# Loading a pair's keys and values: two 64-partition transfers, or one over 128 partitions and a small one for the tail

## The chip, the cores and the metric

The kernel runs on one core of one Trainium2 chip. The metric is the device time of one execution in microseconds (us), the median of several runs; lower is better. Engines are named as in the profile: PE (TensorE matmuls), PEld (its weight loads), DVE (VectorE), ACT (ScalarE), POOL (GpSimd), SP (SyncE, which issues every DMA here).

## What is computed

Two stages. The first is linear attention over 8 batches of 8 heads, 576 tokens and head dimension 64; its normed output, with the heads side by side, is the input x of the second, a gated feed-forward block with a spatial mixing of the 576 tokens.

```python
kv = np.einsum('bhsd,bhse->bhde', k, v)
out = np.einsum('bhsd,bhde->bhse', q, kv)
rms = np.sqrt(np.mean(out * out, axis=-1, keepdims=True) + 1e-06)
x = heads_side_by_side(out / rms * g_norm)         # 8 x 576 x 512

h = np.maximum(x @ w_in, 0.0)                      # 512 -> 1024
u, v = h[..., :512], h[..., 512:]
v_n = (v - mu) / np.sqrt(var + 1e-06)              # over the 512
v_s = np.einsum('ts,bsd->btd', w_spatial, v_n) + b_spatial[None, :, None]
out = (u * v_s) @ w_out                            # 512 -> 512
```

All inputs are float32 except `w_in` and `w_out`, which come as 64-bit floats.

## The kernel before

**Attention.** Heads go in pairs (`p`, four to a batch), so that a pair fills 128 columns. 576 tokens are four chunks of 128 (`NC = 4`) and a tail of 64 (`TAIL`). `att_load` (L97) brings a pair's keys and values into one of two `KV` buffers of shape `[P, 2, NC + 1, P]`: key or value, chunk, column. The fifth chunk is the tail in partitions 0 to 63, with zeros in 64 to 127 set once at the start. The host lays the tail beside the four chunks for partitions 0 to 63 (`kvlo`, 320 KB a pair) and leaves the four chunks alone for 64 to 127 (`kvhi`, 256 KB), so a pair takes two transfers of 64 partitions each; the very first pair takes four, in two pieces. `att_k` (L116) forms the 64x64 product of each head of the pair in ten matmuls (five chunks, two heads) into `pskv` and copies it to `KVB` (even batches) or `KVO` (odd ones). `att_qa` multiplies it with the queries (`qt`, or `qs` for the tail rows), `norm_a` and `norm_b` are the RMS norm (line 169 its sums, line 174 its product), `att_t` transposes to `XH` and its rounding rest `XL`. The tails of two batches are handled together (`pst`, `pstt`).

**Feed-forward.** All big products are float32r in a high and a low part, so three matmuls each. `hv_k`/`hv_end` make `v` (`psh`), normalise it and split it into `VH`, `VL` with the sums (L312 to L315) that a Strassen-like spatial product needs; `u_unit` makes `u` (`psu`, evicted by ACT into `U` at L343); `sp_steps` is the spatial product with the gate (`psa`, `psb`, `psc`), `out_unit` the last product. `psh`, `psu`, `psa`, `psb` and `psc` share four banks.

**Weights** are loaded to `stage` buffers and split: `weight64` (L484) with ACT, DVE and POOL for `w_in` and `w_out` (to `WIH`, `WIL`, `WOH`, `WOL`), `make_ws` and `make_tail` for `wsT`, the transposed spatial weights (to `WSH`, `WSL`, `WTH`, `WTL`). POOL works in pieces of 144 columns.

**Order.** Over the first two batches the order is written out by hand in `PLAN` (W loads a weight, C converts one, L loads the next of the attention's inputs, K and J are `att_k`, A/D and B the norm's two halves, T transposes, H one step of `psh`, u a `psu` unit, s a spatial step). Later batches interleave attention steps of the batches to come with the feed-forward of this one. The kernel is built with a scheduler that orders each engine's instructions by its own estimate of times, so instructions move where an estimate changes. At most two pairs' keys are in flight (`issue`, L569), and all DMAs are issued by SP in order.

Of the kernel before, what the change touches and what calls it, by code (L numbers as in the profile page):

```python
# [8 lines left out]
F32 = mybir.dt.float32  # L9
# [7 lines left out]
B, H, S, D = 8, 8, 576, 64  # L17
DM, FF = 512, 1024
FH = FF // 2
P = 128  # L20
NP = H // 2
NC = S // P
TAIL = S - NC * P
# [20 lines left out]


@with_exitstack
def body(ctx: ExitStack, tc, qT, kvlo, kvhi, g2, w_in, wsT, bsp, w_out, out):
    nc = tc.nc
    w_in = w_in.bitcast(U32)
    w_out = w_out.bitcast(U32)  # L50
# [9 lines left out]
    def persistent(shape, dt, name):  # L60
        return const.tile(shape, dt, name=name, tag=name)
# [21 lines left out]
    KVO = [persistent([P, P], F32, f"KVO{i}") for i in range(NP)]  # L83


    KV = [persistent([P, 2, NC + 1, P], F32, f"KV{i}") for i in range(2)]
    ident = persistent([P, P], F32, "ident")
    gcol = persistent([P, 1], F32, "gcol")
    epsc = persistent([P, 1], F32, "epsc")
# [4 lines left out]
    keys, queries = {}, {}  # L94
    n_load = [0]

    def att_load(b, p, kind):  # L97
        if kind in "fk":
            kv = KV[n_load[0] % 2]
            n_load[0] += 1  # L100
            for i, j in ((0, 2), (2, NC + 1)) if (b, p) == (0, 0) else ((0, NC + 1),):
                nc.sync.dma_start(kv[0:TAIL, :, i:j], kvlo[b, p, :, :, i:j])
                j = min(j, NC)
                nc.sync.dma_start(kv[TAIL:P, :, i:j], kvhi[b, p, :, :, i:j])
            keys[b, p] = kv, None
        if kind == "k":
            qs = load.tile([P, P], F32, name="qs", tag="qs")
            nc.sync.dma_start(qs, qT[b, p, :, S - P:S])
            keys[b, p] = kv, qs
        else:  # L110
            n = S if kind == "f" else NT
            qt = load.tile([P, S], F32, name="qt", tag="qt")
            nc.sync.dma_start(qt[:, 0:n], qT[b, p, :, 0:n])
            queries[b, p] = qt

    def att_k(b, p, st, copy=nc.vector.tensor_copy):  # L116
        kv, qs = keys.pop((b, p))
        ps = ps_att.tile([P, 512], F32, name="pskv", tag="att")

        for c in range(NC + 1):  # L120
            for h in slice(0, D), slice(D, P):
                nc.tensor.matmul(ps[h, h], kv[:, 0, c, h], kv[:, 1, c, h],  # L122
                                 start=c == 0, stop=c == NC)
        st[p] = KVO[p] if b % 2 else KVB[p % 2]
        copy(st[p][0:D, 0:D], ps[0:D, 0:D])
        nc.scalar.copy(st[p][D:P, D:P], ps[D:P, D:P])
        if qs is not None:
            att_end(p, st, qs)
        issue()

    def att_end(p, st, q):

        if p == 0:
            st["tail"] = ps_tail.tile([P, 512], F32, name="pst", tag="tail")
        nc.tensor.matmul(st["tail"][:, p * P:(p + 1) * P], q, st[p], start=True, stop=True)  # L135
# [92 lines left out]
    def att_steps(b):  # L228

        st = states.setdefault(b, {})  # L230

        def loading(f):
            return lambda: (f(), ahead())

        def t2():
            att_t(b, 2, st)
            tail_a(b, st)
            tail_b(b, st)

        def tail():  # L240
            tail_a(b, st)
            tail_b(b, st)

        K = [lambda p=p: att_k(b, p, st) for p in range(NP)]
        Q = [loading(lambda p=p: att_q(b, p, st)) for p in range(NP)]
        T = [lambda p=p: att_t(b, p, st) for p in range(NP)]
        end = lambda: att_tail(b, st)
        if b % 2 == 0:
            return [K[0], K[1], Q[0], K[2], Q[1], T[0], K[3], Q[2], T[1], Q[3], t2, T[3], end], []
        return [loading(k) for k in K] + [tail, end], [Q[0], Q[1], T[0], Q[2], T[1], Q[3], T[2],  # L250
                                                       T[3], move_tail]
# [317 lines left out]
    def issue():  # L569

        while wanted[0] and todo and (len(queries) if todo[0][2] == "q" else len(keys)) < 2:
            wanted[0] -= 1
            att_load(*todo.pop(0))
# [6 lines left out]
    nc.vector.memset(epsc, EPS)  # L580
    nc.scalar.activation(small.tile([P, 1], F32, name="warm", tag="av"), epsc, AF.Sqrt)
    nc.gpsimd.memset(KVB[0], 0.0)
    for kv in KV:
        nc.gpsimd.memset(kv[TAIL:P, :, NC, :], 0.0)
    for kvb in KVO:
        nc.gpsimd.memset(kvb, 0.0)
    make_identity(nc, ident)
# [32 lines left out]
    def conv():  # L620
# [12 lines left out]
        "N": warm,  # L633
        "L": lambda: ahead(), "W": lambda: loads.pop(0)(), "C": conv, "S": step,
        "K": lambda b, p: att_k(b, p, st[b]), "A": lambda b, p: att_qa(b, p, st[b]),
        "B": lambda b, p: att_qb(b, p, st[b]), "T": lambda b, p: att_t(b, p, st[b]),
        "J": lambda b, p: att_k(b, p, st[b], nc.scalar.copy),
        "D": lambda b, p: att_qa(b, p, st[b], True), "d": lambda b: tail_a(b, st[b], True),
        "a": lambda b: tail_a(b, st[b]), "b": lambda b: tail_b(b, st[b]),
# [95 lines left out]
```

## Time and profile before

| | |
|---|---|
| median of 3 runs | 540.55 us (537.82 to 540.96) |
| span of the profiled execution | 538.6 us; no other time is given for it, and the median lies 1.95 us above the span |
| PE busy | 510.0 us, 95% of the span |
| DVE, ACT, POOL busy | 370.7, 247.1, 92.8 us |
| DMA | 46.7 MB, 31.6% of 16 engines' span |
| keys and values | 31 issues each of 320.0 KB (5.4 us to landing) and 256.0 KB (5.8 us), beside the first pair's four smaller ones |

Busy time is the time in which an engine executes. Idle time of an engine counts only where another waits for it. The granted PE clock is a share of full speed. The table of stretches gives for each piece of the span the busy time of every engine; a timeline row gives start, duration, engine, line, operation, out<-in, and in brackets the idle time before it with what ended it.

### The profile page before, as it was taken

Reading aid. Unit: us, or ns where it says so; the run is one execution under the profiler, and the core shown is the slowest. Engines: PE = TensorE matmul, PEld = TensorE weight load, DVE = VectorE, ACT = ScalarE, POOL = GpSimd, SP = SyncE. Lnnn points to the kernel's source line nnn. Section 1 sums busy time; section 2 is a strip of 40 time slices with the busy share of each in tenths; the row PEclk is TensorE's granted clock in tenths of the full one; section 3 lists DMA queues with packets and bytes.
Section 4 is the critical chain, followed back from the end, with each engine's and each line's share of the span. In section 5 each row is a group of like instructions: output and inputs, shape, how many; then the busy total and the mean of one; then the engine's idle time right before and its main releaser. Section 6 shows DMA issues by size and latency. Waiting matters only on the chain.

```text
span 538.6 us, 9728 instructions
## 1 busy us (share of the span) xinstructions
PE 510.0 (95%) x3568; PEld 459.2 (85%) x3568; DVE 370.7 (69%) x1086; ACT 247.1 (46%) x645; POOL 92.8 (17%) x181
## 2 busy tenths in 40 slices
PE   6958787999999999999999999999999999999997
PEld 5747776989897899989998799978998789988995
DVE  2898879888494497918585289928577089947470
ACT  4675864355442356425444256424444256434421
POOL 7699995323000000000000000000000000000000
PEclk7896798999999999999999999999999999999999
DMA  8995412062517401120733800120451500010002
GB/s 232 289 297 127 115 39 63 22 175 58 153 34 178 116 2 40 44 79 2 158 101 86 211 21 21 44 79 0 116 135 50 157 8 12 21 60 19 2 2 97
DMA packets 22344, 46.68 MB, mean 87 GB/s; under 512 B 2900, under 2 KB 5460, under 8 KB 22296
## 3 DMA queue, kind: packets, MB, share of 16 engines
q1 hardware_dynamic: 22296, 46.06, 31.6%
q8 instruction: 28, 0.46, 0.4%
q14 instruction: 20, 0.16, 0.1%
HBM read 36.61 MB, written 9.44 MB: 85 GB/s over the span
## 4 chain that ended last, share of the span: by engine, by line
PE 80%; DMA 10%; DVE 5%; POOL 1%; SPq 1%; issue 1%; ACT 1%; POOLq 0%; DVEq 0%
PE psu L258 19%; PE pso L258 16%; PE psh L288 15%; PE psb L352 6%; PE pso L182 4%; PE psa L352 4%; PE psc L352 4%; PE pskv L122 4%; DMA KV<-kvlo 3%; DMA KV<-kvhi 3%; DMA stage<-w_in 2%; PE pstr L210 2%; PE psh L258 2%; DMA stage<-wsT 1%; PE pst L135 1%
## 5 line engine op out<-in xcount | busy, mean ns | idle before, releaser
L258 PE MATMUL psu<-XH,WIH 128*128 128x288 f32 x256 | 77.7, 304 | 3.6 <-ACT U L343 3.6
L258 PE MATMUL psu<-XL,WIH 128*128 128x288 f32 x256 | 76.4, 299 | 0.0
L258 PE MATMUL psu<-XH,WIL 128*128 128x288 f32 x256 | 76.2, 299 | 0.0
L258 PE MATMUL pso<-WOH,GH 128*128 128x512 f32 x144 | 59.1, 410 | 0.1
L226 POOL CAST XL<-XL 128x256 fp32r<-128x256 f32 x4 | 2.0, 507 | 324.0 <-PE psu L258 324.0
L258 PE MATMUL pso<-WOL,GH 128*128 128x512 f32 x144 | 57.1, 396 | 0.0
L379 ACT CAST GH<-g 128x288 fp32r<-128x288 f32 (+2 forms) x96 | 30.0, 351 | 53.3 <-DVE g L371 48.8
L258 PE MATMUL pso<-WOH,GL 128*128 128x512 f32 x144 | 54.4, 397 | 0.0
L267 DVE BATCH_NORM_STATS2 s<-v 128x6 f32<-128x512 f32 x36 | 24.7, 691 | 42.7 <-ACT v L264 42.5
L258 PEld LDWEIGHTS psu<-XH,WIH 128*128 128x128 f32 x256 | 49.1, 192 | 4.7 <-ACT U L343 3.9
L288 PE MATMUL psh<-WIH,XH 128*128 128x512 f32 x128 | 51.7, 404 | 0.0
L288 PE MATMUL psh<-WIL,XH 128*128 128x512 f32 x128 | 51.3, 401 | 0.0
L258 PEld LDWEIGHTS psu<-XL,WIH 128*128 128x128 f32 x256 | 49.1, 192 | 0.2
L258 PEld LDWEIGHTS psu<-XH,WIL 128*128 128x128 f32 x256 | 48.9, 192 | 0.0
L288 PE MATMUL psh<-WIH,XL 128*128 128x512 f32 x128 | 48.5, 395 | 0.0
L292 DVE TENSOR_TENSOR VL<-v,VH 128x512 fp32r<-128x512 f32 (+1 forms) x64 | 39.8, 639 | 7.1 <-ACT VH L291 6.7
L343 ACT ACTIVATE U<-psu 128x288 f32<-128x288 f32 x64 | 26.2, 411 | 36.6 <-PE psu L258 35.6
L453 ACT COPY o<-pso 128x512 f32<-128x512 f32 x35 | 19.8, 588 | 45.8 <-PE pso L258 43.7
L291 ACT CAST VH<-v 128x512 fp32r<-128x512 f32 (+1 forms) x64 | 34.8, 565 | 11.7 <-DVE v L271 5.5
L169 DVE TENSOR_REDUCE ss<-x 128x8 f32<-128x512 f32 x35 | 23.9, 682 | 20.2 <-ACT x L168 19.8
L122 PEld LDWEIGHTS pskv<-KV 128*64 128x64 f32 x640 | 23.6, 146 | 15.0 <-issue 8.3
L122 PE MATMUL pskv<-KV 128*64 128x64 f32 x640 | 28.4, 237 | 7.5 <-DMA KV<-kvhi 5.1
(144 smaller groups left out, 1309.0 us busy)
## 6 DMA issues: line engine op xcount, KB each, us to landing
KV<-kvlo SPq DMA_DIRECT2D x31, 320.0 KB, 5.4
out<-o SPq DMA_DIRECT2D x32, 256.0 KB, 2.1
KV<-kvhi SPq DMA_DIRECT2D x31, 256.0 KB, 5.8
qt<-qT SPq DMA_DIRECT2D x16, 288.0 KB, 3.1
stage<-w_in SPq DMA_DIRECT2D x8, 512.0 KB, 8.9
qt<-qT SPq DMA_DIRECT2D x16, 256.0 KB, 2.7
stage<-w_out SPq DMA_DIRECT2D x4, 512.0 KB, 4.2
stage<-wsT SPq DMA_DIRECT2D x4, 288.0 KB, 7.7
```

What stands on the lines that cost most here:

```text
L122: nc.tensor.matmul(ps[h, h], kv[:, 0, c, h], kv[:, 1, c, h], start=c == 0, stop=c == NC)
L169: nc.vector.tensor_reduce(ss, heads(x), axis=AX.X, op=ALU.add)
L182: nc.tensor.matmul(ps[:, c * P:(c + 1) * P], qt[:, c * P:(c + 1) * P], st[p], start=True, stop=True)
L258: nc.tensor.matmul(ps, lt, rh, start=i == 0, stop=i == n - 1)
L267: nc.vector.bn_stats(s6, v)
L288: nc.tensor.matmul(ps, lt, rh, start=k == 0 and i == 0, stop=k == NP - 1 and i == 2)
L291: nc.scalar.copy(hi, x)
L292: nc.vector.tensor_tensor(lo, x, f32(hi), op=ALU.subtract)
L343: nc.scalar.activation(U[:, d, cols], ps[:, 0:HS], AF.Relu)
L352: nc.tensor.matmul(ps, lt, rh, start=start and i == 0, stop=stop and i == len(pairs) - 1, skip_group_check=True)
L379: nc.scalar.copy(GH[:, d, dst], g[:, src])
L453: nc.scalar.copy(o, ps)
```

## The change

The four chunks of a pair come as one transfer over all 128 partitions (`kvm`, 512 KB), and the 64 tail tokens as a second one (`kvt`, 64 KB) to a tile of their own, `KT`, of which there are two as of `KV`. `KT` holds zeros in partitions 64 to 127. The host lays the arrays out to match. The first pair still comes in pieces: two chunks, two chunks, tail.

```diff
-    KV = [persistent([P, 2, NC + 1, P], F32, f"KV{i}") for i in range(2)]
+    KV = [persistent([P, 2, NC, P], F32, f"KV{i}") for i in range(2)]
+    KT = [persistent([P, 2, P], F32, f"KT{i}") for i in range(2)]
...
-            kv = KV[n_load[0] % 2]
+            kv, kt = (x[n_load[0] % 2] for x in (KV, KT))
             n_load[0] += 1
-            for i, j in ((0, 2), (2, NC + 1)) if (b, p) == (0, 0) else ((0, NC + 1),):
-                nc.sync.dma_start(kv[0:TAIL, :, i:j], kvlo[b, p, :, :, i:j])
-                j = min(j, NC)
-                nc.sync.dma_start(kv[TAIL:P, :, i:j], kvhi[b, p, :, :, i:j])
-            keys[b, p] = kv, None
+            for i, j in ((0, 2), (2, NC)) if (b, p) == (0, 0) else ((0, NC),):
+                nc.sync.dma_start(kv[:, :, i:j], kvm[b, p, :, :, i:j])
+            nc.sync.dma_start(kt[0:TAIL], kvt[b, p])
+            keys[b, p] = kv, kt, None
...
         for c in range(NC + 1):
+            of = kv[:, :, c] if c < NC else kt
             for h in slice(0, D), slice(D, P):
-                nc.tensor.matmul(ps[h, h], kv[:, 0, c, h], kv[:, 1, c, h],
+                nc.tensor.matmul(ps[h, h], of[:, 0, h], of[:, 1, h],
                                  start=c == 0, stop=c == NC)
...
-    for kv in KV:
-        nc.gpsimd.memset(kv[TAIL:P, :, NC, :], 0.0)
+    for kt in KT:
+        nc.gpsimd.memset(kt[TAIL:P], 0.0)
```

The scheduler moves instructions on every engine over the first 125 us or so of the program; behind that, PE's order is nearly the same. Lines of the change stand one higher than before from L102 on (L343 becomes L344, and so on). Three places matter below.

On SP, at the loads for the last two `wsT` rows and the first two pairs of batch 2 (about 48 to 55 us in the profile), there stood before:

```order
L515 DMA stage<-wsT 128x576
L108 DMA qs<-qT 128x128 x2
L104 DMA KV_98<-kvhi 64x2x512
L102 DMA KV_98<-kvlo 64x1280
L102 DMA KV_99<-kvlo 64x1280
L104 DMA KV_99<-kvhi 64x2x512
L515 DMA stage<-wsT 128x576
```

and now:

```order
L516 DMA stage<-wsT 128x576
L108 DMA qs<-qT 128x128 x2
L516 DMA stage<-wsT 128x576
L103 DMA KV_98<-kvm 128x1024
L104 DMA KT_100<-kvt 64x256
L103 DMA KV_99<-kvm 128x1024
L104 DMA KT_101<-kvt 64x256
```

The last `wsT` has moved ahead of the two pairs, which wait for matmuls that free their buffers.

On ACT, from the first `VH` cast of batch 0 (`VH` is the high part of the normalised v) to the first eviction of `U` (about 55 to 61 us), before:

```order
L291 CAST VH<-v 128x256
L291 CAST VH<-v 128x512
L144 ACTIVATE sv<-mv,epsc 128x1
L526 CAST WSH<-stage 128x288
L165 ACTIVATE x,ss<-pst 128x64 x8
L526 CAST WSH<-stage 128x288 x2
L343 ACTIVATE U<-psu 128x288 x2
```

and now:

```order
L292 CAST VH<-v 128x256
L292 CAST VH<-v 128x512
L145 ACTIVATE sv<-mv,epsc 128x1
L527 CAST WSH<-stage 128x288
L166 ACTIVATE x,ss<-pst 128x64 x8
L527 CAST WSH<-stage 128x288
L292 CAST VH<-v 128x512
L145 ACTIVATE sh<-ss,epsc 128x8
L292 CAST VH<-v 128x256
L527 CAST WSH<-stage 128x288
L292 CAST VH<-v 128x512
L344 ACTIVATE U<-psu 128x288 x2
```

Three more `VH` casts stand ahead of the first eviction of `U`.

On DVE, at the layer norm of batch 0's fourth chunk (`rv`, `v`, `VL`) and the norms of batch 1's attention (`ss`, `rh`, `x`), about 70 to 76 us, before:

```order
L169 TENSOR_REDUCE ss<-x 128x8
L153 SCALAR_TENSOR_TENSOR rv<-qv,rv 128x1
L145 TENSOR_SCALAR ah<-ss 128x8
L271 TENSOR_SCALAR v<-v,mv,rv 128x512
L146 RECIPROCAL qh<-ah 128x8
L151 TENSOR_TENSOR rh<-sh,qh 128x8
L152 SCALAR_TENSOR_TENSOR qh<-sh,rh 128x8
L169 TENSOR_REDUCE ss<-x 128x8
L153 SCALAR_TENSOR_TENSOR rh<-qh,rh 128x8
L292 TENSOR_TENSOR VL<-v,VH 128x512
L145 TENSOR_SCALAR ah<-ss 128x8
L174 TENSOR_TENSOR x<-pso,rh 128x512
```

and now:

```order
L154 SCALAR_TENSOR_TENSOR rv<-qv,rv 128x1
L272 TENSOR_SCALAR v<-v,mv,rv 128x512
L293 TENSOR_TENSOR VL<-v,VH 128x512
L313 TENSOR_TENSOR v<-v 128x256
L205 SCALAR_TENSOR_TENSOR XL<-pstt,gcol,XH 128x4x64
L314 TENSOR_TENSOR v<-v 128x256
L315 TENSOR_TENSOR v<-v 128x256
L316 TENSOR_TENSOR v<-v 128x256
L293 TENSOR_TENSOR VL<-v,VH 128x512 x2
L268 BN_STATS s_968<-v 128x6
L170 TENSOR_REDUCE ss<-x 128x8
```

The fourth chunk's whole chain to `VL` now comes first, and the two norms of batch 1 (L169, now L170) behind it.

More of the change, by code (lines that the diff above doesn't have):

```diff
@@ L46, in body @@
 @with_exitstack
-def body(ctx: ExitStack, tc, qT, kvlo, kvhi, g2, w_in, wsT, bsp, w_out, out):
+def body(ctx: ExitStack, tc, qT, kvm, kvt, g2, w_in, wsT, bsp, w_out, out):
     nc = tc.nc
@@ L108, in att_load @@
             nc.sync.dma_start(qs, qT[b, p, :, S - P:S])
-            keys[b, p] = kv, qs
+            keys[b, p] = kv, kt, qs
         else:
@@ L116, in att_k @@
     def att_k(b, p, st, copy=nc.vector.tensor_copy):
-        kv, qs = keys.pop((b, p))
+        kv, kt, qs = keys.pop((b, p))
         ps = ps_att.tile([P, 512], F32, name="pskv", tag="att")
         for c in range(NC + 1):
+            of = kv[:, :, c] if c < NC else kt
             for h in slice(0, D), slice(D, P):
-                nc.tensor.matmul(ps[h, h], kv[:, 0, c, h], kv[:, 1, c, h],
+                nc.tensor.matmul(ps[h, h], of[:, 0, h], of[:, 1, h],
                                  start=c == 0, stop=c == NC)
@@ L703, in rows @@
         main = a[:, :, :NC * P].reshape(B, NP, NC, P, P).transpose(0, 1, 3, 2, 4)
-        tail = a[:, :, NC * P:].reshape(B, NP, TAIL, 1, P)
-        return np.concatenate([main[:, :, :TAIL], tail], axis=3), main[:, :, TAIL:]
-    klo, khi = rows(k)
-    vlo, vhi = rows(v)
+        return main, a[:, :, NC * P:]
+    km, kt = rows(k)
+    vm, vt = rows(v)
     g = np.asarray(g_norm).reshape(D, 1)
@@ L713 @@
         "qT": np.asarray(q).reshape(B, NP, 2, S, D).transpose(0, 1, 2, 4, 3).reshape(B, NP, P, S),
-        "kvlo": np.stack([klo, vlo], axis=3),
-        "kvhi": np.stack([khi, vhi], axis=3),
+        "kvm": np.stack([km, vm], axis=3),
+        "kvt": np.stack([kt, vt], axis=3),
         "g2": np.concatenate([g, g], axis=0),
```

## The prediction

> **What bounds the kernel now.** I read the page's head first, then the table of stretches, then the chain of waits.
>
> ```profile
> span 538.6 us, 9728 instructions
> PE 510.0 (95%) x3568; PEld 459.2 (85%) x3568; DVE 370.7 (69%) x1086; ACT 247.1 (46%) x645; POOL 92.8 (17%) x181
> ```
>
> ```profile
> 15.00:30.00 15.00, 13.07 (x101) 10.74 (x99) 13.11 (x31) 9.96 (x33) 11.16 (x20) 0.89 1.04 310
> 30.00:45.00 15.00, 6.91 (x58) 5.48 (x59) 12.74 (x29) 9.89 (x47) 15.00 (x27) 0.79 0.83 214
> 45.00:60.00 15.00, 11.99 (x99) 10.58 (x98) 14.50 (x38) 8.83 (x35) 15.00 (x30) 0.84 0.75 185
> 60.00:75.00 15.00, 14.36 (x90) 14.19 (x91) 10.56 (x28) 12.70 (x30) 14.79 (x30) 0.80 0.14 33
> 75.00:90.00 15.00, 10.22 (x67) 8.92 (x65) 14.68 (x36) 8.12 (x18) 12.37 (x22) 0.99 0.18 48
> 90.00:100.00 10.00, 9.39 (x52) 9.01 (x51) 8.42 (x23) 3.43 (x9) 0.00 (x0) 0.67 0.17 56
> ```
>
> The columns are the stretch, its length, busy time of PE, PEld, DVE, ACT and POOL, granted PE clock, DMA share and GB/s. Of the 28.6 us in which PE is idle (538.6 less 510.0), 19.1 lie in these 85 us. Nothing but waits can be taken away, since the change adds and removes no matmul: a pair still has ten per half, two of which now read KT. From 15 to 60 us three resources are full at once: the DMA engines (share 1.04, 0.83, 0.75), POOL (15.00 of 15) and DVE (13.11, 12.74 and 14.50 of 15, so 4.65 us idle). The chain says which of them is waited for:
>
> ```profile
> 19.91 11.39 DMA stage<-w_in
> 31.36 11.43 DMA KV<-kvlo
> 53.48 6.01 DMA stage<-wsT
> 59.51 0.77 ACT WSH L526 x2
> 60.28 0.32 ACT U L343
> ```
>
> A load takes over 11 us to land here because it stands behind others. Between 20 and 60 us the chain runs through transfers for 28.8 us.
>
> **The transfers.** How fast they go depends on how many partitions they write:
>
> ```profile
> 30.00:33.75 3.75, 3.41 (x32) 2.87 (x32) 3.22 (x7) 2.68 (x19) 3.75 (x7) 1.00 1.04 393
> 33.75:42.50 8.75, 1.43 (x6) 0.72 (x4) 8.72 (x21) 7.00 (x28) 8.75 (x15) 0.78 0.95 189
> 166.00:171.50 5.50, 5.50 (x44) 4.37 (x43) 1.45 (x4) 1.60 (x4) 0.00 (x0) 1.00 1.01 227
> ```
>
> In the first row w_in arrives, over 128 partitions: 393 GB/s. In the other two mostly KV does, over 64: 189 and 227 GB/s, with the engines just as full (0.95, 1.01). I take 393 and 227. A pair's 589,824 bytes cost 2.60 us before; afterwards 524,288 bytes at 393 cost 1.33 and the tail's 65,536 at 227 cost 0.29, together 1.62. That is **1.0 us less of all DMA engines for each pair**. The load at 31.36 is the sixth pair, so it would find the backlog about 6 us shorter. The bounds: nothing, if the rates come from what ran beside the transfers, and 1.4 us a pair at 189 GB/s (3.12 less 1.68).
>
> [...]
>
> **Term 1, the start.** PE's first two waits for keys:
>
> ```profile
> 6.20 0.45 PE L122 MATMUL pskv<-KV 128*64 128x64 f32 x8 [1.46 <-DMA KV<-kvhi]
> 7.74 0.78 PE L122 MATMUL pskv<-KV 128*64 128x64 f32 x12 [1.08 <-DMA KV<-kvhi]
> ```
>
> The first pair comes in two pieces. By the rates each piece is 0.5 us shorter (262,144 bytes: 1.15 to 0.67; then 327,680 bytes: 1.44 to 0.96), so the second wait ends 1.0 us sooner. I carry this 1.0 into every chain behind it; the bounds are 0 and 1.0, since an engine with other work may give it back.
>
> **Term 2, the middle.**
>
> ```profile
> 39.44 1.09 PE L210 MATMUL pstr<-ident,x 128*128 128x128 f32 x4 [5.36 <-DVE x L174]
> 42.93 1.33 PE L122 MATMUL pskv<-KV 128*64 128x64 f32 x20 [2.40 <-DMA KV<-kvlo]
> 28.17 0.49 DVE L490 TENSOR_SCALAR t<-t 128x512 uint32<-128x512 uint32 x1 [0.42 <-ACT t L489]
> 32.03 0.55 DVE L490 TENSOR_SCALAR t<-t 128x512 uint32<-128x512 uint32 x1 [0.28 <-ACT t L489]
> 44.37 0.22 DVE L125 COPY KVO<-pskv 64x64 f32<-64x64 f32 x1 [1.70 <-POOL stage L482]
> ```
>
> The 2.40 us wait of PE goes with a backlog 6 us shorter. But the matmul ahead of it waited 5.36 us for DVE, which is nearly full, so what counts is DVE's idle time that came from transfers: 1.70 at the copy of pskv (put down to POOL, but it reads the matmul of 42.93) and 0.42 and 0.28 at weights. With term 1 DVE is 1.0 + 1.7 + 0.7 = 3.4 us ahead at about 49 us. From 45 to 60 us it is busy for 14.50 of 15, up to the next place where PE stops:
>
> ```profile
> 60.64 0.61 PE L258 MATMUL psu<-XH,WIH 128*128 128x288 f32 x1 [3.65 <-ACT U L343]
> 60.19 0.70 ACT L343 ACTIVATE U<-psu 128x288 f32<-128x288 f32 x2
> 60.49 0.41 DVE L315 TENSOR_TENSOR v<-v 128x256 f32<-128x256 f32 x1
> L291 ACT CAST VH<-v 128x512 fp32r<-128x512 f32 (+1 forms) x64 | 34.8, 565 | 11.7 <-DVE v L271 5.5
> 54.00 1.65 POOL L482 TENSOR_TENSOR WIL<-stage 128x144 fp32r<-128x144 f32 x4
> 61.22 4.81 POOL L482 TENSOR_TENSOR WSL<-stage,WSH 128x144 fp32r<-128x144 f32 x8
> ```
>
> PE has no bank left until ACT evicts U. In the old order that eviction stood behind WSH, whose wsT landed at 59.5; wsT is now issued ahead of the next pairs, so this wait goes. Its place is taken by another: the new order puts three VH casts ahead of the first U, and the last needs DVE's L315, which ended at 60.90. In the old times U would start at 60.90 + 0.57 = 61.47, 1.28 later than the 60.19 of before. Less 3.4 this is 58.07, **2.1 us sooner**. POOL must not be later: its last piece of WIL ended at 55.65; six more pieces (0.41 to 0.60 us each, say 0.5) now stand ahead of it: 58.65, less term 1 57.65, just early enough. Bounds: 1.28 us slower with DVE where it was, and 4.4 faster with all 4.65 us of DVE's idle gone and term 1 whole (1.0 + 4.65 - 1.28).
>
> **Term 3, 75 to 90 us.** PE is idle for 4.78 us there, and DVE busy for 14.68 of 15.
>
> ```profile
> 78.99 0.40 PE L352 MATMUL psb<-WSH,VH 128*128 128x288 f32 x1 [0.78 <-ACT VH L291]
> 80.85 0.40 PE L352 MATMUL psb<-WSH,VL 128*128 128x288 f32 x1 [1.32 <-DVE VL L292]
> ```
>
> The new DVE order computes VL ahead of two norms of the odd batch that stood before it. These two waits, 2.1 us, should go; the norms move back, and what needs them is then later. I take 1.0, half. Bounds: 0 and 4.78, and below nothing the same 2.1 given back and once more, since a full engine can only exchange work.
>
> **Term 4, three later stalls**, at the last pair of batches 2, 4 and 6:
>
> ```profile
> 172.12 0.80 PE L122 MATMUL pskv<-KV 128*64 128x64 f32 x20 [0.41 <-DMA KV<-kvhi]
> 300.32 0.80 PE L122 MATMUL pskv<-KV 128*64 128x64 f32 x20 [0.36 <-DMA KV<-kvhi]
> 424.08 0.80 PE L122 MATMUL pskv<-KV 128*64 128x64 f32 x20 [0.22 <-DMA KV<-kvhi]
> ```
>
> Two pairs load together there: 2.0 us less, more than any of the waits. They sum to **1.0**; bounds 0 and 1.0. From about 125 us on, PE's order is the same but for a matmul here and there, and PE is full, so I count nothing else. Memsets are two of the same size; SP issues one transfer less, off the path.
>
> **The sum**: 2.1 (term 1 is in it) + 1.0 + 1.0 = 4.1 us. The profiled execution shows a span of 538.6, and the median of the three timed runs is 1.95 above it (540.55; the lowest is 537.82). I leave that 1.95 as it is: 540.55 - 4.1 = **536.4**.
>
> **Rivals.**
>
> The clock comes up too. PE had 0.80 of its clock from 60 to 75 us (3.0 us lost) and 0.67 from 90 to 100 (3.3 lost), each after stretches with idle PE. If the shorter stalls spare the second and a third of the first, the time is 536.4 - 4.3 = 532.1. For it: the 3.65 us stall loses its cause. Against: PE still does little from 30 to 45 us. [...] Chance 0.27.
>
> What is won is given back: DVE at 14.68 of 15 from 75 to 90 us finishes the odd batch's norms when it did before, and only term 4 is left: 539.5. For it speaks that row; against it DVE's 4.4 us of idle time from 60 to 75. Chance 0.20.
>
> Slower: the U eviction behind the VH casts. If DVE is less than 1.28 us ahead at L315 (a wait for a weight that ACT's new order puts earlier would be enough), PE's stall of 3.65 grows by up to 1.28, and the low clock after it, 3.0 us of loss now, by half again, 1.5. Less term 4: 540.55 + 1.3 + 1.5 - 1.0 = 542.3. It decides at an L315 that ends after 59.6. Chance 0.10.
>
> The change doesn't do what it says: a small transfer holds the engines far longer than its bytes.
>
> ```profile
> qs<-qT SPq DMA_DIRECT2D x1, 64.0 KB, 1.9
> ```
>
> If the tail held them for the whole 1.9 us that the like-sized qs took to land, a pair would cost 3.2 instead of 2.6, 3.6 us over six pairs; with two thirds of it on the path, 543. Against: at 227 to 393 GB/s the bytes of qs take 0.17 to 0.29 us of that time. Chance 0.05.
>
> **How the numbers follow.** The forecast has 0.38 and covers 534 to 538.5. The range must take in most of the clock case and the slower one's middle: 530.5 to 542.5. A measurement of this kernel can tell about 1% (5.4 us) from no change: faster by more is the clock case and the forecast's better edge, 0.35; slower by more needs the slower cases with more than their price, 0.08; within it 0.57.
>
> **What would show it.** The new KV rows should move near 390 GB/s; the sixth pair's matmul should follow its pstr without a wait for a transfer, before 40 us; the first U eviction should start near 58 and directly behind a VH cast; no pskv wait past 0.1 us at the later last pairs; PE's idle time to 100 us some 3 us less. I am wrong if KV's rate stays near 227, if POOL shows as what PE waits for, or if PE's work after 100 us changes.

## The result and the profile after

The kernel after the change took **542.18 us** (median of 20 runs), the kernel before 539.21 us on the same chip (20 runs): ratio **1.0054, 95% interval 1.0033 to 1.0074**. The change made the kernel slower by 1.8 to 4.0 us; 4.1 us less had been forecast. (The 540.55 us that the forecast starts from is 1.3 us above this median of before, so the forecast time of 536.4 us is nearer to the measured one than the forecast change is.) Beside the kernels of the experiments both were run again: 541.75 against 539.33 us, ratio 1.0045 (1.0019 to 1.0071). The first profile of the kernel after fell on an execution of 991.24 us, in which PE is busy for 977.1 us; so all lines of "after" come from a second one, whose execution took 543.52 us, above the median of its 12 runs (540.07 to 545.71).

The page of after, head and DMA queue (packets, MB, share of 16 engines' span):

```profile
span 541.7 us, 9727 instructions
PE 510.8 (94%) x3568; PEld 458.7 (85%) x3568; DVE 372.0 (69%) x1086; ACT 246.2 (45%) x645; POOL 93.2 (17%) x181
q1 hardware_dynamic: 22344, 46.06, 26.6%
```

The same queue of the kernel before:

```profile
q1 hardware_dynamic: 22296, 46.06, 31.6%
```

The transfers did what the change is for. The same 46.06 MB took 31.6% of 538.6 us before, 170.2 us, and take 26.6% of 541.7 us now, 144.1 us: 26.1 us less over 32 pairs, **0.82 us a pair**. PE is idle for 30.9 us (541.7 less 510.8), 2.3 us more than before, and the table of stretches says where (stretch, length, busy time of PE, PEld, DVE, ACT and POOL, granted PE clock, DMA share, GB/s):

```profile
15.00:30.00 15.00, 12.18 (x88) 9.21 (x87) 13.33 (x30) 9.72 (x33) 11.93 (x21) 0.90 1.04 378
30.00:45.00 15.00, 11.19 (x80) 8.77 (x80) 14.66 (x32) 11.53 (x50) 15.00 (x25) 0.89 0.46 138
45.00:60.00 15.00, 8.50 (x87) 7.59 (x87) 13.03 (x39) 9.57 (x39) 15.00 (x29) 0.96 0.46 135
60.00:75.00 15.00, 12.30 (x74) 11.88 (x74) 10.40 (x20) 8.90 (x19) 15.00 (x30) 0.81 0.08 22
75.00:90.00 15.00, 13.17 (x79) 11.86 (x78) 13.19 (x33) 8.28 (x18) 12.11 (x24) 0.87 0.23 61
90.00:100.00 10.00, 8.89 (x49) 8.38 (x49) 8.39 (x22) 3.43 (x9) 0.00 (x0) 0.68 0.15 45
100.00:115.00 15.00, 11.66 (x62) 9.36 (x60) 14.11 (x37) 5.48 (x13) 6.31 (x13) 1.00 0.20 55
130.00:500.00 370.00, 369.83 (x2610) 333.70 (x2609) 252.72 (x788) 163.47 (x392) 3.80 (x8) 1.00 0.23 72
```

From 15 to 30 us the loads run at 378 GB/s instead of 310, and from 30 to 45 us the DMA engines are busy for 0.46 of the time instead of 0.83. From 30 to 45 us PE is idle for 3.81 us instead of 8.09. Then the gain is lost twice: from 45 to 60 us PE is idle for 6.50 instead of 3.01 us, and from 100 to 115 us, where it had not been idle at all, for 3.34 us. That last stretch before:

```profile
100.00:115.00 15.00, 15.00 (x102) 12.19 (x100) 13.20 (x34) 6.29 (x15) 5.83 (x11) 1.00 0.30 80
```

The waits of after that stand there (PE's timeline, idle time and releaser in brackets):

```profile
59.25 0.85 PE L259 MATMUL psu<-XH,WIL 128*128 128x288 f32 x2 [5.15 <-POOL WIL L483]
61.00 0.61 PE L259 MATMUL psu<-XH,WIL 128*128 128x288 f32 x1 [0.91 <-POOL WIL L483]
61.41 0.44 PE L259 MATMUL psu<-XH,WIH 128*128 128x288 f32 x1
105.32 0.50 PE L289 MATMUL psh<-WIH,XH 128*128 128x512 f32 x1 [0.96 <-DVE g L370]
115.23 0.63 PE L211 MATMUL pstr<-ident,x 128*128 128x128 f32 x4 [2.01 <-DVE x L175]
```

PE waits for POOL at the place where it had waited for ACT's eviction of U, and from 105 us on for what DVE makes. The matmul at 61.41 is the one that stood at 60.64 us before (the first that needs the bank that U's eviction frees): **the point where PE goes on is 0.8 us later than before**, where the forecast had it 2.1 us sooner. It serves below as a mark, since the same matmuls stand ahead of it in all kernels, in nearly the same order.

### The profile page after: what moved, and what is told of

It reads as the page before. It is cut to its first block, busy times and chain, and to the rows that moved or that the text cites. A ratio compares the mean times of both kernels' runs of the same rounds, so it can differ in the third digit from the quotient of the medians.

```text
span 989.5 us, 9727 instructions
## 1 busy us (share of the span) xinstructions
PE 977.1 (99%) x3568; PEld 808.5 (82%) x3568; DVE 375.8 (38%) x1086; ACT 246.2 (25%) x645; POOL 86.6 (9%) x181
## 3 DMA queue, kind: packets, MB, share of 16 engines
q1 hardware_dynamic: 22344, 46.06, 14.3%
## 4 chain that ended last, share of the span: by engine, by line
PE 98%; ACT 1%; DMA 1%; SPq 0%; issue 0%; DVE 0%; ACTq 0%
PE pso L259 21%; PE psu L259 20%; PE psh L289 18%; PE psb L353 8%; PE pso L183 6%; PE psa L353 5%; PE psc L353 5%; PE pskv L123 4%; PE pstr L211 3%; PE psh L259 2%; PE pst L136 1%; PE psc L359 1%; PE psc L361 1%; PE pstt L218 1%; DMA KV<-kvm 1%; PE psb L361 0%
## 5 line engine op out<-in xcount | busy, mean ns | idle before, releaser
L259 PE MATMUL psu<-XH,WIH 128*128 128x288 f32 x256 | 120.0, 470 | 3.5 <-ACT U L344 3.5
L259 PE MATMUL psu<-XL,WIH 128*128 128x288 f32 x256 | 120.0, 469 | 0.0
L259 PE MATMUL psu<-XH,WIL 128*128 128x288 f32 x256 | 119.0, 467 | 0.0
L259 PE MATMUL pso<-WOH,GH 128*128 128x512 f32 x144 | 99.3, 690 | 0.0
L259 PE MATMUL pso<-WOL,GH 128*128 128x512 f32 x144 | 97.7, 679 | 0.0
L259 PE MATMUL pso<-WOH,GL 128*128 128x512 f32 x144 | 94.4, 679 | 0.0
L344 ACT ACTIVATE U<-psu 128x288 f32<-128x288 f32 x64 | 26.3, 414 | 147.8 <-PE psu L259 147.8
L259 PEld LDWEIGHTS pso<-WOH,GL 128*128 128x128 f32 x144 | 43.7, 305 | 21.2 <-issue 19.3
L259 PEld LDWEIGHTS pso<-WOH,GH 128*128 128x128 f32 x144 | 43.4, 301 | 18.5 <-issue 15.9
L259 PEld LDWEIGHTS pso<-WOL,GH 128*128 128x128 f32 x144 | 43.2, 300 | 17.4 <-issue 16.1
L289 PEld LDWEIGHTS psh<-WIH,XH 128*128 128x128 f32 x128 | 38.4, 300 | 20.5 <-issue 17.8
```

The lines of the kernel that those rows point to most:

```text
L259: nc.tensor.matmul(ps, lt, rh, start=i == 0, stop=i == n - 1)
L289: nc.tensor.matmul(ps, lt, rh, start=k == 0 and i == 0, stop=k == NP - 1 and i == 2)
L344: nc.scalar.activation(U[:, d, cols], ps[:, 0:HS], AF.Relu)
```

## The experiments

The scheduler orders each engine anew when the transfers change, so the change is two things: other transfers, and another order. To part them, a kernel's order can be fixed: behind the program's body a function chains every engine's instructions, each to the one that is to come before it, in a given order and without any semaphore of its own. (No kernel was run that is held in its own order throughout, which would show what holding costs by itself.)

```diff
     with tile.TileContext(nc, schedule_with_timeline_sim=True) as tc:
         body(tc, *args)
+        pin(tc, ORDER)    # ORDER: for each engine, its instructions in the order wanted
```

Theory A: the transfers are worth about what was forecast, and the new order costs more. Rival B: the new transfers themselves bring little or harm.

**The kernel after, again** (no edit).

> The changed kernel again, beside the kernel before, for a profile of an undisturbed execution. All theories: 2 to 4 us over the kernel before (ratio 1.003 to 1.007). To be read from its trace: where PE's idle time of the first 100 us lies, whether the sixth pair still waits for its load, and what ends the wait at the first eviction of U.

541.75 us, ratio 1.0045 (1.0019 to 1.0071): the result stands.

**The new transfers in the old order.**

```diff
-(the order that the scheduler gives after.py)
+ORDER = that of before.py, on all five engines
```

> The new transfers, with every engine's instructions held in the order that they have in the kernel before (a pair's two transfers in the two places of the old ones). Theory A, the transfers are worth what the prediction says and the scheduler's new order costs more: 2 to 5 us faster than before (ratio 0.990 to 0.996), keys' waits of PE before 45 us down from about 5 us to under 2. Theory B, the shorter transfers are hidden behind DVE and POOL, and the new order costs the whole difference: 1.000 within 0.002. Theory C, the new transfers cost by themselves (the tail lands late): 1.004 to 1.007, and PE or SP waits for KT.

535.50 us, ratio **0.9926 (0.9900 to 0.9952)**: 3.8 us faster than before, and the fastest kernel of this study. PE's waits for WIL, and two stretches:

```profile
55.10 0.53 PE L259 MATMUL psu<-XH,WIL 128*128 128x288 f32 x2 [2.28 <-POOL WIL L483]
56.83 0.40 PE L259 MATMUL psu<-XH,WIL 128*128 128x288 f32 x1 [1.20 <-POOL WIL L483]
15.00:30.00 15.00, 13.94 (x122) 11.20 (x122) 14.86 (x33) 10.85 (x41) 12.43 (x21) 1.00 0.98 357
100.00:115.00 15.00, 15.00 (x112) 12.26 (x111) 13.18 (x40) 6.75 (x17) 7.34 (x16) 1.00 0.34 110
```

PE's waits for keys before 45 us fall from 6.5 us in before to 2.2. Even in the old order POOL becomes what PE waits for, but for 3.48 instead of 6.06 us; the mark is at 57.39 us, and from 100 to 115 us PE is never idle.

**The old transfers in the new order.**

```diff
-(the order that the scheduler gives before.py)
+ORDER = that of after.py, on all five engines
```

> The old transfers, with every engine's instructions held in the order of the changed kernel. Theory A: slower than the changed kernel, 1.010 to 1.020 of before, since the new order has lost the shorter transfers. Theory B: like the changed kernel, 1.004 to 1.007. Theory C: 1.000 within 0.002.

544.89 us, ratio **1.0092 (1.0061 to 1.0123)**.

```profile
60.49 0.67 PE L258 MATMUL psu<-XH,WIL 128*128 128x288 f32 x2 [4.46 <-POOL WIL L482]
100.00:115.00 15.00, 11.59 (x68) 9.27 (x68) 13.33 (x35) 5.28 (x13) 7.32 (x15) 1.00 0.18 55
```

Both stalls of after are there with the old transfers, the mark at 62.51 us. The median lies just under the range of theory A (1.010 to 1.020) and above that of B, and its interval reaches into both; what decides for A is the pair of comparisons, which agree: the transfers are worth 3.1 us in the new order (544.89 less 541.75) and 3.8 us in the old one (539.33 less 535.50); the order costs 5.6 us with the old transfers and 6.3 us with the new ones.

**Where the order costs.** Two kernels with the new transfers change from one order to the other at the third eviction of U, about 62 us. A third changes at 95 us.

```diff
-ORDER = that of after.py
+ORDER = after.py's first 216 PE, 117 DVE, 109 ACT, 99 POOL and 41 SP instructions, then the rest as in before.py
```

> The new transfers; every engine follows the new order up to the third eviction of U (about 62 us), and before's order from there on. Theory 1 (the new order costs in two places of about 3 us each, POOL's late last piece of WIL at 53 to 61 us and the norms of batch 1 that reach PE at 100 to 115 us): PE still waits 5 to 6 us for WIL, its 3.3 us of idle time at 100 to 115 us are gone, 538.5. Theory 2 (all of the loss arises in the first 62 us, and what PE lacks later only follows from it): 541.7 as the new order. Theory 3 (the late WIL is made up for later, the norms alone cost): 535.5.

538.94 us, ratio 0.9993 (0.9973 to 1.0013). The wait for WIL is there and the second stall is not:

```profile
59.02 0.85 PE L259 MATMUL psu<-XH,WIL 128*128 128x288 f32 x2 [5.09 <-POOL WIL L483]
100.00:115.00 15.00, 15.00 (x104) 12.40 (x103) 13.24 (x34) 6.00 (x16) 5.27 (x10) 1.00 0.31 91
```

```diff
-ORDER = that of after.py
+ORDER = before.py's first 216 PE, 113 DVE, 105 ACT, 93 POOL and 45 SP instructions, then the rest as in after.py
```

> The new transfers; before's order up to the third eviction of U, the new order from there on. Theory 1: PE's wait for WIL is about 3.5 us as in the kernel with before's order throughout, its idle time at 100 to 115 us is there (about 3.3 us), 538.5. Theory 2: 535.5. Theory 3: 541.7.

540.06 us, ratio 1.0019 (0.9998 to 1.0039), 1.6 us above what theory 1 gave. The second stall is there:

```profile
100.00:115.00 15.00, 12.27 (x91) 9.92 (x90) 11.42 (x30) 5.18 (x13) 6.00 (x14) 0.89 0.24 66
```

Against the old order throughout (0.9926), the new first part costs 0.67% or 3.6 us, the new second part 0.93% or 5.0 us, and both together (1.0045) 1.19% or 6.4 us. Both places cost, as theory 1 has it, and by the medians 2.2 us are common to both. Four ratios enter that number, each known to 0.2 or 0.3%, so it isn't clear of noise.

```diff
-ORDER = that of after.py
+ORDER = after.py's instructions up to 95 us (366 PE, 174 DVE, 144 ACT, 141 POOL, 53 SP), then the rest as in before.py
```

> The new transfers; the new order up to 95 us, before's order from there on. In the new order's trace DVE makes the norms of batch 1 at 79 to 84 us, where they stand at 67 to 77 us with before's order, and PE later waits for x at 107 and 115 us. Theory: the loss is made by the norms' place ahead of 95 us and only shows behind it, so the time stays near 541. Rival (PE's order from 95 us on, which asks for the third transpose of x too early, makes it): PE is busy for 15.0 of 15 us from 100 to 115, 539 as with the switch at 62 us.

540.44 us, ratio 1.0020 (0.9997 to 1.0042). By the time alone this is unclear, since the interval overlaps that of after and that of the change at 62 us. The trace says more:

```profile
98.10 0.63 PE L211 MATMUL pstr<-ident,x 128*128 128x128 f32 x4 [2.41 <-DVE GL L381]
90.00:100.00 10.00, 5.75 (x45) 5.14 (x44) 8.93 (x24) 3.77 (x9) 0.00 (x0) 1.00 0.25 82
100.00:115.00 15.00, 15.00 (x107) 12.59 (x106) 13.50 (x36) 5.88 (x16) 4.41 (x8) 1.00 0.29 93
```

With before's order behind 95 us the idle time only moves forward: 4.25 us from 90 to 100 us and none after (DVE's x, which the transposes at 98.10 read, ends at 97.95, just before the GL that the row names). So in this execution what is missing is missing before 95 us, where the new order has the norms of batch 1. The first of their sums on DVE, in after and in before:

```profile
79.63 0.69 DVE L170 TENSOR_REDUCE ss<-x 128x8 f32<-128x512 f32 x1 [0.16 <-ACT x L169]
```

```profile
70.82 0.67 DVE L169 TENSOR_REDUCE ss<-x 128x8 f32<-128x512 f32 x1
```

They are 8.8 us later, and PE's waits from 105 us on are for what DVE makes behind them. Not all of the 8.8 us is the order. Ahead of the norms the profile of after has one DVE step that lasts 3.57 us instead of 0.69, beside an unbroken row of POOL's pieces:

```profile
69.94 3.57 DVE L293 TENSOR_TENSOR VL<-v,VH 128x512 fp32r<-128x512 f32 x1 [1.87 <-ACT VH L292]
71.55 0.96 POOL L483 TENSOR_TENSOR WSL<-stage,WSH 128x144 fp32r<-128x144 f32 x2
72.45 1.40 POOL L483 TENSOR_TENSOR WTL<-stage,WTH 64x144 fp32r<-64x144 f32 x2
```

That is 2.9 of the 8.8 us. Such a step is in the profiles of after_to_95 (2.99 us) and of the old transfers in the new order (3.45) too, but not in those of pool_first and of the kernel that changes to the new order at 62 us, which have the same DVE order there; the table below has it for every kernel, and the last section has what was measured of such steps. Those two are without it and PE is idle there for 2.8 and 2.7 us from 100 to 115 us all the same, so the order is enough for most of the 3.34 us. That it is the norms' place in the order is argued from these rows; no run moved the norms alone.

**POOL's last weight earlier.** The kernel after in its own order, but on POOL:

```diff
 L483 TENSOR_TENSOR stage<-stage,WIH 128x144 x4
+L483 TENSOR_TENSOR WIL<-stage 128x144 x4
 L483 TENSOR_TENSOR stage<-stage 128x144 x2
 L483 TENSOR_TENSOR WSL<-stage,WSH 128x144 x4
 L483 TENSOR_TENSOR stage<-stage 128x144 x4
-L483 TENSOR_TENSOR WIL<-stage 128x144 x4
```

> The new kernel in its own order but for one engine: POOL makes its last four pieces of WIL directly behind the four subtractions they need, ahead of ten pieces of wsT. They would end near 54 us in place of 60.95. Theory 1, first place: PE's waits for WIL (5.15 and 0.91 us) go, and 3 us are gained, 538.7, if nothing takes their place. Rival (the VH and WSH casts that stand ahead of U's first eviction on ACT take over, since the pieces of wsT that WSH reads are now about 1.9 us later): U's first eviction stays at 59.9 us or later, PE waits for it instead, 541 to 542.

541.26 us, ratio 1.0032 (1.0010 to 1.0053): no gain that can be told from after, as the rival had it. POOL, ACT (cast, eviction) and PE:

```profile
51.40 2.30 POOL L483 TENSOR_TENSOR WIL<-stage 128x144 fp32r<-128x144 f32 x4
59.06 0.43 ACT L527 CAST WSH<-stage 128x288 fp32r<-128x288 f32 x1 [2.04 <-POOL stage L483]
61.27 0.70 ACT L344 ACTIVATE U<-psu 128x288 f32<-128x288 f32 x2
61.72 0.61 PE L259 MATMUL psu<-XH,WIH 128*128 128x288 f32 x1 [7.56 <-ACT U L344]
```

WIL ends at 53.7 instead of 60.95 us and PE no longer waits for it, but U's first eviction stands on ACT behind a WSH cast that waits for POOL's pieces of wsT, and behind VH casts; it starts 1.4 us later than in after (61.27 against 59.90), and PE waits for that instead, until the mark at 61.72 us. Two chains end near 60 us, and with one shortened PE waits for the other.

**The two chains at once, from the fastest kernel.** POOL's last four pieces of WIL behind the pieces of the weight before, and U's first evictions ahead of two WSH casts (wil_u_first), or of all three (u_ahead):

```diff
 (ACT, new transfers in the old order)
 L527 CAST WSH<-stage 128x288         (u_ahead: this cast moved behind the new L344)
 L166 ACTIVATE x,ss<-pst 128x64 x8
+L344 ACTIVATE U<-psu 128x288 x2      (both kernels)
 L527 CAST WSH<-stage 128x288 x2
-L344 ACTIVATE U<-psu 128x288 x2
```

> The kernel with the new transfers and before's order, with two edits: POOL makes the last four pieces of WIL directly behind the eight pieces of the weight before it (ahead of two pieces of wsT and four of WSL), and ACT evicts U twice ahead of the two WSH casts that wait for wsT. There PE waited 2.28 and 1.20 us for WIL. If that place bounds the kernel, 2 to 3 us are gained: 532.5 to 533.5. Rival (DVE, which is full from 45 to 60 us, bounds what comes behind it): 535.5, with PE's idle time moved to a later place.

536.85 us, ratio 0.9954 (0.9935 to 0.9973): neither the gain nor the 535.5 us of the rival.

> As wil_u_first, but ACT evicts U twice ahead of all three WSH casts that wait for POOL or for wsT, directly behind the eight products of the norm. There PE waited 3.54 us for the eviction, which started at 58.2 us though psu was full by 55.2. Theory: the eviction starts near 55.5, the wait falls under 1 us, and the time to 533 to 534. Rival (DVE, which makes what PE needs from 75 us on, bounds the stage whatever PE does at 58): PE waits longer at 75 to 90 us, 535.5 to 536.

536.55 us, ratio 0.9948 (0.9927 to 0.9969). In wil_u_first PE waits 3.54 us for U and the mark is at 58.72, later than the 57.39 of the kernel it starts from: the eviction stood behind the eight products of the norm, and these behind a WSH cast that waited 2.94 us for POOL. In u_ahead the mark is at 55.70 us, 1.7 sooner, and the time is none the less no better (0.9948 against 0.9926). So an earlier mark alone brings nothing here. What sets the end was not settled: the profiled execution of u_ahead was the longest of its 12, 541.03 us where the median is 536.55, and has a DVE step of 5.30 us instead of 0.16, shown in the last section.

**What the transfers' gain is made of.** The four chunks in two transfers of 64 partitions, the tail still by itself, the order still before's:

```diff
-                nc.sync.dma_start(kv[:, :, i:j], kvm[b, p, :, :, i:j])
+                nc.sync.dma_start(kv[0:TAIL, :, i:j], kvm[b, p, 0:TAIL, :, i:j])
+                nc.sync.dma_start(kv[TAIL:P, :, i:j], kvm[b, p, TAIL:P, :, i:j])
```

> The kernel with the new transfers and before's order, with one edit: the four chunks come as two transfers of 64 partitions each (kvm's upper and lower 64), the tail in its own as in the change; the bytes are the same, the order of all else too. Theory A (the change pays by writing 128 partitions at once): the first 45 us move at about before's rate, and the time is near before's, 538 to 539. Rival B (it pays by what comes with it, a tail out of the way of the chunks, or two columns of loads fewer): 535.5, as with one transfer.

537.88 us, ratio 0.9987 (0.9963 to 1.0011): the time of before.

```profile
q1 hardware_dynamic: 22872, 46.06, 31.4%
15.00:30.00 15.00, 12.88 (x106) 10.25 (x107) 12.88 (x29) 9.79 (x33) 11.24 (x21) 1.00 1.06 310
```

The DMA engines are busy again for 31.4% of the span and move 310 GB/s from 15 to 30 us, as in the kernel before (31.6%, 310 GB/s); with one transfer in the same order it was 26.5% and 357 GB/s. So what the transfers save comes from writing 128 partitions in one transfer. By the medians most of the gain in time goes with it. Why it goes isn't shown: in the profiled execution, among the quickest of the 12 (536.36 us, span 534.6), PE waits for keys for 2.3 us before 45 us, as little as with one transfer.

The kernel with the new transfers in the old order, without the tail's transfer (so the keys and values of the last 64 tokens are left out):

```diff
-            nc.sync.dma_start(kt[0:TAIL], kvt[b, p])
-        nc.gpsimd.memset(kt[TAIL:P], 0.0)
+        nc.gpsimd.memset(kt, 0.0)
```

> The kernel with the new transfers and before's order, without the tail's transfer (KT holds zeros, so 64 of the 576 tokens are missing from the keys and values; the matmuls are the same). By the bytes a tail costs 0.29 us of all DMA engines, 1.7 us over six pairs, of which only what PE or DVE waits for counts: 535 to 535.5. Rival (a small transfer holds the engines for far longer than its bytes): 533 or less.

536.01 us, ratio 0.9944 (0.9925 to 0.9962): not faster than with the tail (0.9926). No run shows that the tail takes time.

All kernels in one table: the mark, DVE's longest step from 60 to 80 us, PE's idle time from 60 to 115 us and the span, all of the profiled execution, and the ratio of the medians to before:

| kernel | mark, us | DVE's longest step, us | PE idle, us | span, us | ratio |
|---|---|---|---|---|---|
| before | 60.64 | 0.98 | 6.0 | 538.6 | 1 |
| after, again | 61.41 | 3.57 | 9.0 | 541.7 | 1.0045 |
| new transfers, old order | 57.39 | 0.98 | 6.1 | 533.8 | 0.9926 |
| old transfers, new order | 62.51 | 3.45 | 9.0 | 543.8 | 1.0092 |
| new order to 62 us, then old | 61.18 | 1.75 | 6.2 | 537.5 | 0.9993 |
| old order to 62 us, then new | 58.14 | 1.04 | 7.3 | 539.2 | 1.0019 |
| new order to 95 us, then old | 62.59 | 2.99 | 9.4 | 538.6 | 1.0020 |
| pool_first | 61.72 | 0.98 | 8.7 | 538.4 | 1.0032 |
| wil_u_first | 58.72 | 1.05 | 5.8 | 535.9 | 0.9954 |
| u_ahead | 55.70 | 5.30 | 10.6 | 539.3 | 0.9948 |
| two_halves | 59.14 | 1.06 | 5.5 | 534.6 | 0.9987 |
| no_tail | 56.10 | 4.10 | 8.7 | 535.4 | 0.9944 |

The two slowest kernels have a late mark and much idle time behind it, the fastest has neither. But five of the six rows with 8.7 us of idle time or more hold a DVE step of 2.99 us or more, and two of these, u_ahead and no_tail, are of kernels with an early mark and a low median. The rows are of single executions, and don't give each price to the microsecond.

## Why the prediction was wrong, point by point

**The transfers: right, but for their size.** The step "1.0 us less of all DMA engines for each pair" measured 0.82. The sixth pair's wait of 2.40 us is gone, as forecast:

```profile
40.42 0.69 PE L123 MATMUL pskv<-KV 128*64 128x64 f32 x16
```

So are the waits at the later last pairs: from 130 to 500 us PE is idle for 0.17 us where it was for 1.13 (368.87 busy of 370), so **term 4's 1.0 us** holds. The worth of the transfers with the order held, 3.8 us, is near the sum's 4.1, but that is chance: the sum priced the new order, and two of its terms came out otherwise.

**Term 1: a third of it came.** PE's second wait for keys ends at 7.38 instead of 7.74 us, 0.36 sooner, not 1.0, and the first piece came no sooner (6.40 against 6.20). By PE's next start, at 9.00 instead of 9.09 us, 0.09 is left of it:

```profile
6.40 0.45 PE L123 MATMUL pskv<-KV 128*64 128x64 f32 x8 [1.76 <-DMA KV<-kvm]
7.38 0.47 PE L123 MATMUL pskv<-KV 128*64 128x64 f32 x8 [0.54 <-DMA KV<-kvm]
```

**Term 2: this step failed.** It had two parts, and both came out late. The first is POOL's. The term said of POOL "six more pieces (0.41 to 0.60 us each, say 0.5) now stand ahead of it: 58.65, less term 1 57.65, just early enough". POOL's last piece of WIL ended at 60.95 us. The groups of POOL's work from the second weight to that piece, in before (18.84 to 55.65 us) and after (18.07 to 60.95); each WSL row counts one piece more, which starts as that last piece ends:

```profile
L482 POOL TENSOR_TENSOR stage<-stage,WIH 128x144 f32<-128x144 f32 (+1 forms) x28 | 16.8, 631 | 7.6 <-ACT WIH L492 7.6
L482 POOL TENSOR_TENSOR WIL<-stage 128x144 fp32r<-128x144 f32 (+1 forms) x28 | 13.5, 508 | 0.0
L482 POOL TENSOR_TENSOR WSL<-stage,WSH 128x144 fp32r<-128x144 f32 x7 | 4.8, 698 | 0.0
L482 POOL TENSOR_TENSOR stage<-stage 128x144 f32<-128x144 f32 x6 | 3.3, 567 | 0.0
```

```profile
L483 POOL TENSOR_TENSOR WIL<-stage 128x144 fp32r<-128x144 f32 (+1 forms) x28 | 16.6, 619 | 0.0
L483 POOL TENSOR_TENSOR stage<-stage,WIH 128x144 f32<-128x144 f32 (+1 forms) x28 | 16.2, 610 | 6.8 <-ACT WIH L493 6.8
L483 POOL TENSOR_TENSOR stage<-stage 128x144 f32<-128x144 f32 x10 | 6.0, 619 | 0.0
L483 POOL TENSOR_TENSOR WSL<-stage,WSH 128x144 fp32r<-128x144 f32 x9 | 5.4, 618 | 0.0
```

Before, 68 pieces took 36.8 us, 0.541 each; after, 74 take 42.9 us, 0.579 each. The six more cost 3.25 us at the old length, near the forecast (3.0). But all 74 are 0.038 us longer, 2.8 us together, and the start was 0.77 and not 1.0 us sooner: 57.65 + 0.25 + 0.23 + 2.82 = 60.95. The sum took POOL's speed from the old trace, in which 43 of the 68 pieces had beside them a DVE instruction with two inputs in SBUF (the on-chip memory that holds all tiles here but the ps ones); now 53 of the 74 have, and these last 0.67 us on average, the others 0.48 (the last section has more on this). The second part is DVE's lead. ACT's first eviction of U and the DVE step ahead of it:

```profile
59.90 0.71 ACT L344 ACTIVATE U<-psu 128x288 f32<-128x288 f32 x2 [0.23 <-PE psu L259]
58.21 0.70 DVE L316 TENSOR_TENSOR v<-v 128x256 f32<-128x256 f32 x1
```

DVE's step (L315 before) ended at 58.91 us, 2.0 sooner than before and not 3.4. The eviction stands directly behind a VH cast as forecast and began at 59.90, not 58.07. Only the last 0.23 us were a wait for PE, which waited for POOL: without it the eviction would have begun at 59.67, 1.6 us later than forecast. So with POOL in time the term would still have failed, and pool_first, in which POOL is in time, gains nothing that can be told. The rival "U eviction behind the VH casts" had the place and, with 542.3, nearly the time, but not what decides it: its point, an L315 that ends after 59.6, was not reached. That its time was near is luck: it starts from 540.55 us.

**Term 3: the sign was wrong.** It took 1.0 us, "half" of two waits, and named what would pay for it: "the norms move back, and what needs them is then later". From 75 to 90 us PE's idle time did fall, from 4.78 to 1.83 us. But from 60 to 75 it rose from 0.64 to 2.70, and the norms were asked for at 105 to 115 us, outside the stretch that was looked at: 3.34 us where there had been none. From 60 to 115 us PE's idle time went from 6.03 to 8.98 us. "From about 125 us on, PE's order is the same ... so I count nothing else" left 100 to 125 us uncounted.

**The other rivals.** The clock did not come up (0.80 to 0.81 from 60 to 75 us, 0.67 to 0.68 from 90 to 100); the stall ahead of 60 us grew. The 4.3 us of the clock's rival and the 1.5 us of the slower one take the clock to follow the stalls; that was the author's estimate, and no run shows it by itself: from 60 to 75 us the clock was 0.80 behind a wait of 3.65 us (before), 0.81 behind waits of 5.15 and 0.91 (after), and 0.98 behind 2.28 and 1.20 (the new transfers in the old order). "What is won is given back" named the norms of the odd batch, and had them finished when they were before; they came 8.8 us later. A tail that holds the engines is refuted by the kernel without it (0.9944 against 0.9926 with it). PE's idle time to 100 us is 0.3 us less (23.8 to 23.4), where some 3 had been forecast. The prediction named what would prove the forecast wrong, POOL as what PE waits for and PE's work after 100 us, and both happened.

So the mechanism of the change was right, and about 4 us were there to be had. The order that came with it was priced at 1.28 us in term 2 and a gain of 1.0 in term 3; it cost about 6. That it did is shown by the kernels with a fixed order; how the 6 us divide among POOL's pieces, DVE's lead and the late norms stays open.

## What to carry to other kernels

A change of transfers under a scheduler is two changes; hold the order fixed to see what the transfers bring, and keep the old order if it is better: here that gives 535.5 us instead of 542. A mean piece of POOL's from the old trace was no price for the new one here (0.541 us became 0.579, with 53 of 74 pieces beside a DVE instruction with two inputs in SBUF instead of 43 of 68), and a deferred instruction is to be followed to the place where its result is used, however far. Before a chain is shortened, look for the one that ends beside it: moving POOL's pieces alone brought nothing that could be told, since ACT's eviction was as late.

## What the runs showed of the hardware

**A small product on DVE takes at most 0.16 us without POOL's pieces beside it and up to 5.30 us with them.** The sharpest case is in the profile of u_ahead, DVE and POOL:

```profile
67.93 5.30 DVE L152 TENSOR_TENSOR rv<-sv,qv 128x1 f32<-128x1 f32 x1
67.77 0.49 POOL L483 TENSOR_TENSOR stage<-stage 128x144 f32<-128x144 f32 x1
...
71.40 1.81 POOL L483 TENSOR_TENSOR WTL<-stage,WTH 64x144 fp32r<-64x144 f32 x4
73.27 0.97 POOL L483 TENSOR_TENSOR WTL<-stage,WTL 1x144 fp32r<-1x144 f32 x2
```

A product of 128 single elements lasts 5.30 us, from just after the start of one POOL piece to the first gap in an unbroken row of them (71.40 + 1.81 = 73.21; it ends at 73.23).

In the twelve profiles of the table the same product takes at most 0.16 us in the 362 cases in which nothing of POOL's runs beside it; in the 70 others it takes 0.51 us on average, and 1.75, 4.10 and 5.30 in the three longest. DVE's sum ss, which has one input, takes at most 0.69 us either way (390 and 30 cases). In the other direction, POOL's pieces of 144 columns for WIL take 0.42 us with DVE idle, 0.47 beside other DVE instructions, and 0.67 beside one with two inputs in SBUF (45, 71 and 172 cases). So it isn't DVE's busy time as a whole that tells: from 45 to 60 us POOL ran 30 pieces in before beside 14.50 us of DVE, and 29 in after beside 13.03. These are comparisons within traces; no run kept the two engines apart, so neither the cause nor what it costs a kernel is shown. The nearest figure is u_ahead's, whose execution with the long step was 4.5 us above its median.

**Runs differ in the first 15 us.** PE's granted clock there was 0.76 in the profiles of before and after and 1.00 in that of the new transfers in the old order, with nearly the same work, so kernels are compared here by their medians, and the marks and spans of single executions only with this in mind:

```profile
0.00:15.00 15.00, 10.33 (x74) 9.43 (x75) 4.50 (x13) 6.20 (x26) 10.20 (x29) 0.76 0.86 279
0.00:15.00 15.00, 10.54 (x80) 9.39 (x82) 4.24 (x12) 6.36 (x27) 10.20 (x29) 1.00 0.83 266
```
